# Moving value sums, output products and memory reads between the slots of the last layer

## The chip, the cores and the metric

One core of one Trainium2 chip. The metric is the device time of one execution in microseconds (us), as a median over runs of the same kernel. The core has four compute engines that run side by side: PE (TensorE, the matrix products), DVE (VectorE), ACT (ScalarE) and POOL (GpSimd); SP (SyncE) issues the transfers and, here, also passes on some waits. Results of PE land in PSUM, which this kernel splits into eight banks: four are shared by everything called `g`, two are called `lg`, one `mx`, one `my`.

## What is computed

Four residual layers over x of 2048 rows by 512 columns, 32 heads of 16 columns: linear attention with learned features (A), segment attention with a memory (B), then A and B again with the same weights. Every layer adds its result to x after a layer norm. The change is almost all in B:

```python
for s in range(N):                      # N = 4 segments of L = 512 rows
    qs, ks, vs = q[:, :, s], k[:, :, s], v[:, :, s]
    logits = jnp.einsum("bhqd,bhkd->bhqk", qs, ks) * scale + mask
    p = _softmax(logits, axis=-1)
    a_dot = jnp.einsum("bhqk,bhkd->bhqd", p, vs)
    pq = phi(qs)
    num = jnp.einsum("bhld,bhde->bhle", pq, M)
    den = jnp.einsum("bhld,bhd->bhl", pq, z)[..., None] + 1e-6
    a_mem = num / den
    o = g * a_mem + (1.0 - g) * a_dot   # g = sigmoid(beta), one number per head
    outs.append(o)
    pk = phi(ks)
    M = M + jnp.einsum("bhld,bhle->bhde", pk, vs)
    z = z + jnp.einsum("bhld->bhd", pk)
return o @ wo
```

## The kernel before

**The work of a B layer.** Each segment's 32 heads are worked in eight *half chunks* of four heads. A chunk is 8 heads, that is 128 of the 512 columns, and so two half chunks, `hf` 0 and 1. Half chunks are numbered m = 0 to 31 through a layer; m = 24 to 31 are the last segment's. For each there is a row of five slots (`R = 5`), written m.0 to m.4 with m counted inside the segment (0 to 7).

In every slot PE makes one block of scores into `lg`, ACT takes its exponential into `P`, and POOL cuts `P` along the causal mask (`AFFINE_SELECT`). `lg` holds one block: the next slot's scores wait for this slot's exponential. Beside it PE makes scores for a later half chunk once more, whose row maxima DVE takes (operations with `mask` that write `mxs`): slots .0, .1 and .3 put them in `mx` and `my`, slots .2 and .4 in two `g` tiles (`SPARE`). A transpose `mt<-mxs` then turns the maxima.

**After its five slots a half chunk is summed up.** In slot (m+1).0 PE makes the *value sums* (`weighted`, products of `P` with `v`, 32 matmuls into one `g` tile). ACT *evicts* them from that tile to `U`, scaled by `share`, a number that carries the weight 1 - g of the head (`dve.tensor_scalar(share, ...)` at the start makes it from `gates`). `finish` ("fin" in the tables) lets DVE transpose `U`, take the reciprocal `r` of the sums of exponentials and multiply into `wt`; POOL adds `wt` to `ot`, where the row's share of the memory lies already. That share comes from `reads` ("a0" to "a3", one per chunk): `mem` products into a `g` tile in two rounds, then on DVE a `TENSOR_SCALAR`, a `RECIPROCAL` and a `TENSOR_TENSOR` that reads the bank and writes `ot`.

**The output product.** `convert` ("cv0" to "cv3") transposes a finished chunk of `ot`, ACT copies it to `oh` and DVE or POOL subtracts to get the rest, `ol`. The output product (`out_pair`, "O") takes three products per chunk, `oh` by two parts of `w` and `ol` by one. It runs in `mm3_pair`: two tiles of 128 rows at once, each matmul on 64 of the array's 128 rows, in 24 steps. [...] The change-over is a wait of PE for an empty instruction (`sync.nop`) on SP, which itself waits for PE's last matmul of the part; SP executes in order, so that it stands behind transfers that SP issues before. The last segment's output product is begun early (`early`, "P") on the three chunks that are ready, 18 steps per pair of tiles, and `end` adds the fourth chunk.

**What sets the order.** Four tables written by hand, FIRST, GAPS, LAST and FINAL, name the side work of each slot of a segment: `<` stands ahead of the slot's other work, `O/6` is six steps of the output product, `cv0` the conversion of chunk 0, `pre` the loads of the residual. LAST orders the last segment of the first B layer (layer 1), FINAL that of the second (layer 3, `thin`, the end of the program). In FINAL, rows 2 to 5 hold two output products split by columns into halves of 256 (so 24 steps in each of the four rows).

At the end of the layer m = 31 is summed up: in FINAL by two halves of columns (48 matmuls), ACT evicts each to `U`, `finish` adds both, `end_turn` transposes and splits, `end` multiplies and adds, and the result goes out.

Of the kernel before, what the change touches and what calls it, by code (L numbers as in the profile page):

```python
# [17 lines left out]
DH = 16  # L18
# [72 lines left out]
1.0 <turn <turn <max <a1 | 1.1 fin Q3/6 | 1.2 Q3/6      | 1.3 Q3/6 | 1.4 Q3/6  # L91
2.0 <max <a1 | 2.1 fin O/6          | 2.2 O/6 cv0       | 2.3 O/6 | 2.4 O/6
3.0 <max <a2 | 3.1 fin O/6          | 3.2 O/6           | 3.3 O/6 | 3.4 O/6
4.0 <turn <turn <max <a2 | 4.1 fin O/6 | 4.2 O/6        | 4.3 O/6 cv1 | 4.4 O/6
5.0 <max <a3 | 5.1 fin O/6          | 5.2 O/6           | 5.3 O/6 | 5.4 O/6
6.0 <max <a3 fin pre | 6.1 cv2      | 6.2 P/4           | 6.3 P/9 | 6.4 P/5
7.0 <max | 7.1 fin P/4              | 7.2 P/5           | 7.3 P/4 | 7.4
# [6 lines left out]
def interleave_kernel(ctx, tc, x_in, a_wqkv, a_wphi, a_wo, b_wq, b_wk, b_wv, b_wo, b_beta,  # L104
# [95 lines left out]
    eb = cp.tile([P, H], F32, name="eb")  # L200
    share = cp.tile([P, 8], F32, name="share")
    ones = cp.tile([32, P], F32, name="ones")

    def constants():

        sync.dma_start(out=mask, in_=c_mask)
        sync.dma_start(out=eb, in_=b_beta.unsqueeze(0).broadcast_to([P, H]))
        yield
        yield
        act.activation(eb, eb, AF.Exp, scale=-1.0)  # L210
        dve.tensor_scalar(eb, eb, 1.0, None, op0=ADD)
# [466 lines left out]
    class LayerA:  # L678
# [341 lines left out]
        def pass2(self):  # L1020
# [15 lines left out]
            for i in range(NT):  # L1036
# [31 lines left out]
                if 0 < i <= NT - 4:  # L1068
# [18 lines left out]
    class LayerB:  # L1087
# [261 lines left out]
        def weighted(self, m):  # L1349
# [4 lines left out]
            for w0, w1, kbs in ((0, 256, (0, 1)), (256, 512, (0, 3, 1, 2))) if ends else ((0, 512, (0, 3, 1, 2)),):  # L1354
                pv = PS("g", G)[:, 0 : w1 - w0]
                for kb in kbs:
                    for r in range(2):
                        for e in range(2):
# [6 lines left out]
                            else:  # L1365
# [3 lines left out]
                               lhsT=v[:, kb, h * VW : h * VW + 32], rhs=p[:, q0 - kb * P : w1 - kb * P],  # L1369
                               start=(kb == 0), stop=(kb == kbs[-1]), tile_position=(0, 32 * hh))  # L1370
                U = T2("U", UU)[:, 0 : w1 - w0]
                act.activation(U, pv, AF.Identity, scale=share[:, m % 8 : m % 8 + 1])
                self.U[m].append(U)

        def finish(self, m):
            s, c, hf = m // 8, m % 8 // 2, m % 2
            q0 = 0
            for U in self.U.pop(m):
                n = U.shape[1] // 32
                W = T2("U", UU)[:, 0 : 32 * n]  # L1380
                dve.transpose(out=W, in_=U)
                weigh(self.sums(s, c)[:, q0 : q0 + n, hf : hf + 1],
                      W.rearrange("p (q h e) -> p q h e", q=n, h=1), 0.0, s > 0,
                      dve if m == 8 * NSEG - 1 else pool)
                q0 += n

# [49 lines left out]
        def early(self):  # L1436
# [23 lines left out]

        def end_turn(self):
            s, c = NSEG - 1, NC - 1
            width = 256 if self.thin else 512
            for at in range(0, 512, width):
                S, to = self.turn_sums(s, c, [("oh", OO), ("ol", OO)], ("tb3", TB3), width, at)
                self.split_sums(S, to, dve)

        def end(self):
# [36 lines left out]
        def steps(self, side, after, table_end):  # L1505
# [80 lines left out]
            for s in range(NSEG):  # L1586
                for cell in (FIRST if s == 0 else GAPS if s < NSEG - 1 else table_end).replace("|", "\n").split("\n"):
                    if cell.strip():
                        at_, *what = cell.split()
                        m, j = at_.split(".")  # L1590
                        table[8 * R * s + R * int(m) + int(j)] = what, s
            slots = list(range(*SIDE))
            spent = 0.0
            for k in range(BEGIN, R * N + 1):
# [46 lines left out]
            next(after, None)  # L1641
            self.finish(N - 1)
            for _ in range(4):
                next(early, None)
            for _ in range(2):
                next(after, None)
            self.end_turn()
# [68 lines left out]
```

## Time and profile before

| | |
|---|---|
| runs | 1288.26, 1289.33 and 1291.87 us; median 1289.33 |
| the profiled execution | 1289.33 us, of which the span in the trace is 1287.6 |
| clock of PE granted | 1.00 |
| PE busy | 1253.9 us, 97% of the span |
| DVE, ACT, POOL busy | 83%, 65%, 59% |
| FINAL rows 2 to 5, from PE's value sums of row 2 to those of row 6 | 1213.19 to 1258.09 |
| last value sums of PE end | 1277.44 |

In the rows of the trace a line of "start, us, engine, line, operation, out<-in, count" is one instruction or a run of equal ones, and a bracket at its end is the time the engine was idle just before, with what ended it. Nearly all PE rows bear the line of one helper (L179) and those of the other engines that of another (L157), so a reader goes by the tiles: `g<-P,v` are value sums, `g<-mem,tb` reads, `g<-w,oh`, `g<-w,ol` and `g<-w,x` output products (the conversions of two chunks lie in `x`), `lg<-e,e` scores, and `mx<-e,e`, `my<-e,e`, `g<-e,e` the scores for the maxima. A custom DVE operation with `mask` is a maximum.

### The profile page before, as it was taken

What the parts mean: (1) busy time and instruction counts of PE and PEld (TensorE: products, weight loads), DVE (VectorE), ACT (ScalarE), POOL (GpSimd) and SP (SyncE); (2) the same over time, 40 slices, a digit from 0 to 9 for tenths busy, and PEclk for the clock granted to TensorE, in tenths of its full rate; (3) what the DMA queues carried; (4) which work ended last, traced back from release to release, by engine and by line L of the source; (5) the groups of instructions that cost most, each with busy time, mean ns of one, the idle gap of its engine ahead of it and who ended that gap; (6) DMA issues with size and microseconds to landing.
All of it is one profiled execution on the core that took longest, in us unless ns stands there. A gap on an engine that the chain in (4) does not pass through costs nothing.

```text
span 1287.6 us, 42663 instructions
## 1 busy us (share of the span) xinstructions
PE 1253.9 (97%) x16832; PEld 977.2 (76%) x16832; DVE 1069.0 (83%) x3471; ACT 837.0 (65%) x1258; POOL 753.7 (59%) x1122
## 2 busy tenths in 40 slices
PE   7999999999999999999999999999999999999987
PEld 7887878777777778777668887787877777777765
DVE  5776879699898998999867768887899899899995
ACT  6556446547787787687644434564778967867754
POOL 1668857335667767667324347752456666766653
PEclk9999999999999999999999999999999999999999
DMA  6397348745565545556351102676556545544432
GB/s 216 108 350 259 110 152 259 232 117 151 163 186 150 145 135 145 148 139 170 115 180 51 66 34 83 214 243 173 145 147 203 148 148 138 147 137 118 115 83 83
DMA packets 134423, 196.64 MB, mean 153 GB/s; under 512 B 15440, under 2 KB 61648, under 8 KB 133456
## 3 DMA queue, kind: packets, MB, share of 16 engines
q1 hardware_dynamic: 133408, 193.80, 49.7%
q8 instruction: 134, 2.20, 0.7%
q14 instruction: 65, 0.53, 0.1%
q10 hardware_dynamic: 816, 0.11, 0.1%
HBM read 101.05 MB, written 39.85 MB: 109 GB/s over the span
## 4 chain that ended last, share of the span: by engine, by line
PE 79%; DVE 15%; ACT 2%; issue 1%; DMA 1%; POOL 1%; SPq 0%; DVEq 0%; ACTq 0%; POOLq 0%
PE g L179 61%; PE lg L179 8%; PE g L183 4%; PE mx L179 3%; DVE g L157 3%; DVE mx L157 2%; DVE U L157 2%; DVE my L157 2%; PE my L179 1%; DVE mxs L157 1%; ACT P L157 1%; PE mx L189 1%; DVE es L157 1%; DVE r L157 1%; POOL P L157 1%
## 5 line engine op out<-in xcount | busy, mean ns | idle before, releaser
L157 ACT ACTIVATE P<-lg 128x1024 f32<-128x1024 f32 x316 | 324.2, 1026 | 96.1 <-PE lg L179 76.9
L157 POOL TENSOR_SCALAR_AFFINE_SELECT P<-P 128x256 f32<-128x256 f32 (+1 forms) x448 | 190.0, 441 | 217.3 <-ACT P L157 201.5
L157 DVE CUSTOM_DVE_ANT_0 g<-g,mask 128x128 f32<-128x128 f32 (+3 forms) x392 | 189.5, 538 | 7.3 <-PE g L179 7.0
L157 DVE CUSTOM_DVE_ANT_0 mx<-mx,mask 128x512 f32<-128x512 f32 (+2 forms) x316 | 159.0, 503 | 37.4 <-PE my L179 30.5
L179 PE MATMUL g<-hh,wqk 64*128 64x512 f32 (+1 forms) x960 | 183.6, 392 | 0.4 <-SPq L157 0.2
L179 PE MATMUL g<-w,oh 64*128 64x512 f32 (+2 forms) x848 | 161.8, 380 | 2.6 <-ACT oh L157 2.6
L157 DVE CUSTOM_DVE_ANT_0 my<-my,mask 128x512 f32<-128x512 f32 (+2 forms) x316 | 163.8, 518 | 0.1
L179 PE MATMUL lg<-e,e 64*128 64x512 f32 (+1 forms) x1010 | 146.8, 342 | 7.5 <-ACT P L157 7.5
L179 PE MATMUL g<-P,v 128*32 128x128 f32 (+3 forms) x2064 | 151.7, 433 | 0.2
L157 DVE DVE_READ_ACCUMULATOR2_ANT mxs<- 128x1 f32 x1024 | 143.9, 141 | 0.0
L179 PE MATMUL g<-w,hh 64*128 64x512 f32 (+1 forms) x672 | 142.0, 393 | 0.1
L179 PEld LDWEIGHTS lg<-e,e 64*128 64x128 f32 x1010 | 94.0, 184 | 50.5 <-ACT P L157 19.0
L179 PEld LDWEIGHTS g<-hh,wqk 64*128 64x128 f32 (+1 forms) x960 | 101.1, 185 | 17.2 <-issue 1.0
L179 PEld LDWEIGHTS g<-P,v 128*32 128x32 f32 x2064 | 65.0, 109 | 61.2 <-issue 53.8
L179 PEld LDWEIGHTS g<-w,oh 64*128 64x128 f32 (+1 forms) x848 | 95.6, 186 | 20.2 <-ACT oh L157 3.5
L157 ACT COPY tb<-g 128x512 f32<-128x512 f32 (+1 forms) x132 | 71.1, 575 | 51.5 <-PE g L179 51.3
L179 PE MATMUL g<-hl,wqk 64*128 64x512 f32 (+1 forms) x480 | 102.4, 389 | 0.0
L179 PE MATMUL g<-w,ol 64*128 64x512 f32 (+2 forms) x424 | 100.5, 377 | 0.1
L179 PEld LDWEIGHTS g<-w,hh 64*128 64x128 f32 (+1 forms) x672 | 83.8, 186 | 14.9 <-PE my L179 0.4
L179 PE MATMUL g<-w,hl 64*128 64x512 f32 (+1 forms) x336 | 89.3, 391 | 0.0
L157 POOL TENSOR_TENSOR ta<-tb,ta 128x512 fp32r<-128x512 f32 x60 | 76.2, 1290 | 13.9 <-ACT ta L157 11.0
L179 PE MATMUL g<-e,e 63*128 63x256 f32 (+3 forms) x488 | 83.2, 351 | 0.3 <-issue 0.3
(174 smaller groups left out, 2941.4 us busy)
## 6 DMA issues: line engine op xcount, KB each, us to landing
e<-ta SPq DMA_DIRECT2D x384, 128.0 KB
wqk<-wqk SPq DMA_DIRECT2D x128, 256.0 KB
x<-x SPq DMA_DIRECT2D x48, 256.0 KB
pq<-tb SPq DMA_DIRECT2D x24, 256.0 KB
tb<-pq SPq DMA_DIRECT2D x24, 256.0 KB
x<-xr SPq DMA_DIRECT2D x22, 256.0 KB
xr<-x SPq DMA_DIRECT2D x20, 256.0 KB
x<-in SPq DMA_DIRECT2D x16, 256.0 KB
```

Source lines behind the costliest of these rows:

```text
L157: i = f(*a, **k)
L179: return held(nc.tensor.matmul(*a, **k))
L183: return held(nc.tensor.transpose(*a))
L189: held(nc.tensor.transpose(out, in_[row : row + 64], ident[row : row + 64, row : row + 64], tile_position=(row, 0)))
```

## The change

The tables, `weighted`, `finish` and the end of the layer change, in five parts.

1. **FINAL rows 2 to 5.** The value sums are split over two slots (two of four key blocks in .0, the other two in .1; `parted` lists the half chunks). `fin` goes from .1 to .2. The 24 steps of O go from four slots of 6 to three of 8 (.2, .3, .4), so that the change-overs after steps 6 and 18 now stand in the middle of a slot's steps. The read of each of these rows goes from .0 to .3.
2. **Row 6 of LAST and FINAL.** Value sums in two slots, `fin` from 6.0 to 6.1, the early steps P/4 and P/9 become P/5 and P/8; the first part of P in `mm3_pair` ends after 6 steps instead of 4 (`half`).
3. **The last half chunk (m = 31) of both B layers.** ACT's eviction is left out: DVE transposes straight from PSUM, and the weight is applied in the multiplication (`gate`, kept beside `share`). In FINAL the first half's conversion is done ahead of the second half's, and its second `ol` behind the first result (`low`).
4. **Which engine.** The subtraction of `cv0` and `cv1` in the last segment goes from DVE to POOL (that of `cv2` stays); the addition of `wt` for m = 29 goes from POOL to DVE.
5. **Layers A.** One pair of small scalings, `scale_q`, is issued one step earlier in the second pass.

```diff
 LAST
-6.0 <max <a3 fin pre | 6.1 cv2      | 6.2 P/4           | 6.3 P/9 | 6.4 P/5 v/1
+6.0 <max <a3 pre | 6.1 fin cv2      | 6.2 P/5           | 6.3 P/8 | 6.4 P/5 v/1
 FINAL
-2.0 <max <a1 | 2.1 fin O/6          | 2.2 O/6 cv0       | 2.3 O/6 | 2.4 O/6
-3.0 <max <a2 | 3.1 fin O/6          | 3.2 O/6           | 3.3 O/6 | 3.4 O/6
...
-6.0 <max <a3 fin pre | 6.1 cv2      | 6.2 P/4           | 6.3 P/9 | 6.4 P/5
+2.0 <max | 2.1                      | 2.2 fin O/8       | 2.3 O/8 cv0 a1 | 2.4 O/8
+3.0 <max | 3.1                      | 3.2 fin O/8       | 3.3 O/8 a2 | 3.4 O/8
...
+6.0 <max <a3 pre | 6.1 fin cv2      | 6.2 P/5           | 6.3 P/8 | 6.4 P/5
...
-    def mm3_pair(one, two, kcs=range(NC), closed=True):
+    def mm3_pair(one, two, kcs=range(NC), closed=True, half=None):
-        half = len(terms) // 2
+        half = half or len(terms) // 2
...
         def weighted(self, m):
+                    if m in self.parted and kb == 1:
+                        yield
...
+                if m == 8 * NSEG - 1:
+                    self.U[m].append(pv)
+                    continue
                 U = T2("U", UU)[:, 0 : w1 - w0]
                 act.activation(U, pv, AF.Identity, scale=share[:, m % 8 : m % 8 + 1])
...
+        def last_sums(self):
+            s, c, m = NSEG - 1, NC - 1, 8 * NSEG - 1
+            low = None
+            for n, pv in enumerate(self.U.pop(m)):
+                w = pv.shape[1]
+                q, at = w // 32, w * n
+                W = T2("U", UU)[:, 0:w]
+                dve.transpose(out=W, in_=pv)
+                weigh(self.sums(s, c)[:, at // 32 : at // 32 + q, 1:2], W.rearrange("p (q h e) -> p q h e", q=q, h=1),
+                      0.0, True, dve, gate[:, m % 8 : m % 8 + 1])
+                if low:
+                    low()
+                S, (hi, lo) = self.turn_sums(s, c, [("oh", OO), ("ol", OO)], ("tb3", TB3), w, at)
+                act.copy(hi, S)
+                def low(S=S, hi=hi, lo=lo):
+                    dve.tensor_tensor(out=lo, in0=S, in1=hi.bitcast(F32), op=SUB)
+            return low
...
         def convert(self, s, c):
-            eng = dve if s == NSEG - 1 else pool
+            eng = dve if s == NSEG - 1 and c == NC - 2 else pool
...
+            self.parted = (*(range(N - 7, N - 3) if self.thin else ()), N - 3)
```

**PE, FINAL row 4, slot 4.4.** Before, the scores `lg` are followed by the two score blocks for the maxima and at once by the last six steps of O (two matmuls each):

```order
L179 MATMUL g_21289<-w_15877,ol_20471 128x256
L179 MATMUL g_21288<-w_15877,ol_20471 128x256
L179 MATMUL lg_21374<-e_2112_13208,e_2113_13209 128x256 x4
L179 MATMUL g_21382<-e_2151_13394,e_2150_13393 128x512
L179 MATMUL g_21383<-e_2151_13394,e_2150_13393 128x512
L179 MATMUL g_21288<-w_15877,oh_20024 128x256
```

In the changed kernel the read stands just ahead of that slot's `lg`, and O has eight steps to go:

```order
L179 MATMUL g_21273<-w_15876,oh_20469 128x256
L179 MATMUL g_21272<-w_15876,oh_20469 128x256
L179 MATMUL g_21331<-mem_13202,tb_3351_20506 32x34 x32
L179 MATMUL lg_21368<-e_2111_13207,e_2112_13208 128x256 x4
L179 MATMUL g_21376<-e_2150_13393,e_2149_13392 128x512
L179 MATMUL g_21377<-e_2150_13393,e_2149_13392 128x512
L179 MATMUL g_21273<-w_15877,oh_20469 128x256
```

The read's tile g_21331 and the second tile of the maxima, g_21377, lie in the same bank (with two O tiles and one more tile of maxima, five tiles want four banks), so that g_21377 must wait until DVE has read g_21331.

**DVE, the same place.** Before, a read (`r`, `r`, `ot`) stands early in a row, right behind the turning of the maxima, and no read stands between the maxima of slot .3 and the pair of 512 wide maxima of slot .4; in row 4 only the transpose of `cv1` does:

```order
L157 ISA my_21347,mxs_13204<-my_21347,mask 128x256
L157 ISA mxs_13204 128x1
L157 STREAM_TRANSPOSE U_21372<-ot_20536 128x512
L157 ISA g_21382,mxs_13204<-g_21382,mask 128x512
L157 ISA mxs_13204 128x1
L157 ISA g_21383,mxs_13204<-g_21383,mask 128x512
L157 ISA mxs_13204 128x1
L157 TENSOR_TENSOR x_21371<-U_21372,x_21370 128x512
```

In the changed kernel the read of slot .3 stands between them:

```order
L157 ISA my_21301,mxs_13203<-my_21301,mask 128x256
L157 ISA mxs_13203 128x1
L157 STREAM_TRANSPOSE U_21329<-ot_20535 128x512
L157 TENSOR_SCALAR r_21364<-g_21331 128x16
L157 RECIPROCAL r_21364<-r_21364 128x16
L157 TENSOR_TENSOR ot_21107<-g_21331,r_21364 128x256
L157 ISA g_21376,mxs_13203<-g_21376,mask 128x512
L157 ISA mxs_13203 128x1
L157 ISA g_21377,mxs_13203<-g_21377,mask 128x512
```

What PE waits for at g_21377 is so the `TENSOR_TENSOR ot`, which on DVE stands behind the four 256 wide maxima of the slot and, in the two rows with a conversion, as here, behind its transpose (the row `U_21329<-ot_20535`). The subtraction `x_21371`, which stood ahead of the next row's maxima, has gone to POOL.

**DVE, the end of the program.** Before, both halves of m = 31 are added to `ot` first, from `U` that ACT has evicted, and then turned and split:

```order
L157 STREAM_TRANSPOSE U_21920<-U_21911 128x256
L157 RECIPROCAL r_21922<-U_21920 128x8
L157 TENSOR_TENSOR wt_21924<-U_21920,r_21922 128x128
L157 TENSOR_TENSOR ot_21427<-ot_21427,wt_21924 128x8x16
L157 STREAM_TRANSPOSE tb_3594_21937<-ot_21427 128x256
L157 TENSOR_TENSOR ol_21936<-tb_3594_21937,oh_21935 128x256
L157 STREAM_TRANSPOSE tb_3595_21941<-ot_21427 128x256
L157 TENSOR_TENSOR ol_21936<-tb_3595_21941,oh_21935 128x256
```

In the changed kernel:

```order
L157 STREAM_TRANSPOSE tb_3588_21916<-ot_21540 128x256
L157 STREAM_TRANSPOSE U_21919<-g_21890 128x256
L157 RECIPROCAL r_21921<-U_21919 128x8
L157 SCALAR_TENSOR_TENSOR wt_21923<-U_21919,gate,r_21921 128x128
L157 TENSOR_TENSOR ot_21540<-ot_21540,wt_21923 128x8x16
L157 TENSOR_TENSOR ol_21915<-tb_3588_21916,oh_21914 128x256
L157 STREAM_TRANSPOSE tb_3592_21927<-ot_21540 128x256
L157 TENSOR_TENSOR tb_3539_21672<-g_21941,tb_3539_21672 128x512
L157 TENSOR_TENSOR ol_21915<-tb_3592_21927,oh_21914 128x256
```

The transpose of the first half's sums (`tb_3588`) has moved ahead of the second half's work, the second half is read from the PSUM tile itself, and the first result (`tb_3539`) stands ahead of the last `ol`.

More of the change, by code (lines that the diff above doesn't have):

```diff
@@ L91 @@
 1.0 <turn <turn <max <a1 | 1.1 fin Q3/6 | 1.2 Q3/6      | 1.3 Q3/6 | 1.4 Q3/6
-2.0 <max <a1 | 2.1 fin O/6          | 2.2 O/6 cv0       | 2.3 O/6 | 2.4 O/6
-3.0 <max <a2 | 3.1 fin O/6          | 3.2 O/6           | 3.3 O/6 | 3.4 O/6
-4.0 <turn <turn <max <a2 | 4.1 fin O/6 | 4.2 O/6        | 4.3 O/6 cv1 | 4.4 O/6
-5.0 <max <a3 | 5.1 fin O/6          | 5.2 O/6           | 5.3 O/6 | 5.4 O/6
-6.0 <max <a3 fin pre | 6.1 cv2      | 6.2 P/4           | 6.3 P/9 | 6.4 P/5
+2.0 <max | 2.1                      | 2.2 fin O/8       | 2.3 O/8 cv0 a1 | 2.4 O/8
+3.0 <max | 3.1                      | 3.2 fin O/8       | 3.3 O/8 a2 | 3.4 O/8
+4.0 <turn <turn <max | 4.1          | 4.2 fin O/8       | 4.3 O/8 cv1 a2 | 4.4 O/8
+5.0 <max | 5.1                      | 5.2 fin O/8       | 5.3 O/8 a3 | 5.4 O/8
+6.0 <max <a3 pre | 6.1 fin cv2      | 6.2 P/5           | 6.3 P/8 | 6.4 P/5
 7.0 <max | 7.1 fin P/4              | 7.2 P/5           | 7.3 P/4 | 7.4
@@ L201, in interleave_kernel @@
     share = cp.tile([P, 8], F32, name="share")
+    gate = cp.tile([P, 8], F32, name="gate")
     ones = cp.tile([32, P], F32, name="ones")
@@ L214, in constants @@
         for j in range(4):
-            dve.tensor_copy(share[32 * j : 32 * j + 32, :].rearrange("p (c f) -> p c f", f=2),
+            dve.tensor_copy(gate[32 * j : 32 * j + 32, :].rearrange("p (c f) -> p c f", f=2),
                             gates[32 * j : 32 * j + 32, 0, :].rearrange("p (c j f) -> p j c f", j=4, f=2)[:, j])
-        dve.tensor_scalar(share, share, -1.0, bd[:, 24:25], op0=ADD, op1=MUL)
+        dve.tensor_scalar(share, gate, -1.0, bd[:, 24:25], op0=ADD, op1=MUL)
         dve.tensor_scalar(share, share, 1.0, None, op0=ADD)
@@ L552, in out_pair, with weigh @@
         yield
-    def weigh(out, p, eps, add, eng=pool):
+    def weigh(out, p, eps, add, eng=pool, part=None):
         n, G = out.shape[1], out.shape[2]
@@ L567, in weigh @@
         t = T2("wt", 1, shape=(P, n, G, DH))
-        dve.tensor_tensor(out=t, in0=p[:, :, :, 0:DH], in1=rb, op=MUL)
+        if part is None:
+            dve.tensor_tensor(out=t, in0=p[:, :, :, 0:DH], in1=rb, op=MUL)
+        else:
+            dve.scalar_tensor_tensor(out=t, in0=p[:, :, :, 0:DH], scalar=part, in1=rb, op0=MUL, op1=MUL)
         eng.tensor_tensor(out=out, in0=out, in1=t, op=ADD)
@@ L1081, in pass2 @@
                         yield from transposed(3)
+                    if i == NT - 4:
+                        for f in factors:
+                            scale_q(*f)()
+                        factors = []
                 elif i > NT - 4:
@@ L1373, in weighted @@
                 self.U[m].append(U)
+            yield
         def finish(self, m):
             s, c, hf = m // 8, m % 8 // 2, m % 2
[L1377 to L1385, printed above, removed]
+            U, = self.U.pop(m)
+            W = T2("U", UU)
+            dve.transpose(out=W, in_=U)
+            weigh(self.sums(s, c)[:, :, hf : hf + 1], W.rearrange("p (q h e) -> p q h e", q=16, h=1), 0.0, s > 0,
+                  dve if m == 8 * NSEG - 3 else pool)
+        def last_sums(self):
[15 more added lines that the diff above has]
+            return low
         def turn_sums(self, s, c, tags, src, width=512, at=0):
@@ L1449, in early @@
                 yield from mm3_pair(side(0), side(1), range(NC - 1),
-                                    t == 0 or not self.thin)
+                                    t == 0 or not self.thin, 6)
                 def end(po=po, xs=self.xe[t : t + 2]):
@@ L1459, in early, with end @@
                 yield
[L1461 to L1468, printed above, removed]
+        def end(self, low):
             s = NSEG - 1
@@ L1479, in end @@
                 sync.dma_start(out=self.xdst[4 * s + t], in_=self.xe[t])
+                if low:
+                    low()
+                    low = None
         def opening(self):
@@ L1591, in steps @@
                         table[8 * R * s + R * int(m) + int(j)] = what, s
+            self.parted = (*(range(N - 7, N - 3) if self.thin else ()), N - 3)
+            values = {}
             slots = list(range(*SIDE))
@@ L1621, in steps @@
                 if k % R == 0 and 0 <= k // R - 1 < N:
-                    self.weighted(k // R - 1)
+                    values = self.weighted(k // R - 1)
+                    next(values)
+                elif k % R == 1 and k // R - 1 in self.parted:
+                    next(values)
                 for f in self.rows:
@@ L1641, in steps @@
             next(after, None)
[L1642 to L1647, printed above, removed]
+            low = self.last_sums()
+            if not self.thin:
+                for _ in range(4):
+                    next(early, None)
+                for _ in range(2):
+                    next(after, None)
+                low()
+                low = None
             for _ in early:
@@ L1650, in steps @@
             next(after, None)
-            self.end()
+            self.end(low)
             for f in aside[0]:
```

## The prediction

> **What bounds the kernel now.** I read the page's busy shares and chain first, then busy time by stage, then the rows of PE and DVE over the last 100 us.
>
> ```profile
> span 1287.6 us, 42663 instructions
> PE 1253.9 (97%) x16832; PEld 977.2 (76%) x16832; DVE 1069.0 (83%) x3471; ACT 837.0 (65%) x1258; POOL 753.7 (59%) x1122
> PE 79%; DVE 15%; ACT 2%; issue 1%; DMA 1%; POOL 1%; SPq 0%; DVEq 0%; ACTq 0%; POOLq 0%
> ```
>
> PE is nearly always busy and the chain is mostly PE, so a change can only take out PE's few gaps. The change leaves PE's products as they are, 7567 rows before and after. The gaps stand at the last layer's end; its windows run from value sums to value sums (rows 2 to 7):
>
> ```profile
> core 0: us, PE busy (x) PEld busy (x) DVE busy (x) ACT busy (x) POOL busy (x), PEclk, DMA share, GB/s
> 1213.19:1225.41 12.22, 9.88 (x195) 7.23 (x182) 11.50 (x45) 9.62 (x14) 9.53 (x13) 1.00 0.31 71
> 1225.41:1236.12 10.71, 9.69 (x179) 7.15 (x177) 10.34 (x47) 6.04 (x8) 5.52 (x12) 1.00 0.33 90
> 1236.12:1247.04 10.92, 9.87 (x195) 7.22 (x182) 10.22 (x42) 6.29 (x10) 4.67 (x10) 1.00 0.45 122
> 1247.04:1258.09 11.05, 9.76 (x175) 7.17 (x174) 10.84 (x44) 7.01 (x9) 6.07 (x12) 1.00 0.22 72
> 1258.09:1267.93 9.84, 8.55 (x86) 5.47 (x84) 4.33 (x13) 5.26 (x7) 3.60 (x9) 1.00 0.24 85
> 1267.93:1277.44 9.51, 9.51 (x124) 6.20 (x122) 3.57 (x8) 6.36 (x10) 4.07 (x9) 1.00 0.00 1
> ```
>
> In rows 2 to 5 (44.90 us in all) PE is idle 5.70 us and DVE only 2.00, so DVE sets the pace there. PE's gaps that the change aims at, in both B layers:
>
> ```profile
> 622.67 0.77 PE L179 MATMUL g<-mem,tb 128*32 128x34 f32 x64 [0.63 <-DVE mxs L157]
> 638.54 0.56 PE L179 MATMUL lg<-e,e 64*128 64x256 f32 x4 [1.28 <-ACT P L157]
> 663.62 0.74 PE L179 MATMUL g<-w,oh 128*128 128x512 f32 x2 [1.24 <-ACT oh L157]
> ...
> 1224.67 0.77 PE L179 MATMUL g<-mem,tb 128*32 128x34 f32 x64 [0.94 <-DVE mxs L157]
> ...
> 1262.16 0.56 PE L179 MATMUL lg<-e,e 64*128 64x256 f32 x4 [1.28 <-ACT P L157]
> ...
> 1280.16 0.73 PE L179 MATMUL g<-w,oh 128*128 128x512 f32 x2 [1.35 <-ACT oh L157]
> ```
>
> **FINAL rows 2 to 5.** Here the sign is decided. The order puts the read of slot .3 on DVE behind the four 256 wide maxima, and PE's second 512 wide block of slot .4 into the bank that this read empties. Today DVE runs late and nobody minds. DVE in row 5:
>
> ```profile
> 1247.81 0.29 DVE L157 CUSTOM_DVE_ANT_0 mx<-mx,mask 128x128 f32<-128x128 f32 x1
> ...
> 1249.30 0.84 DVE L157 STREAM_TRANSPOSE mt<-mxs 32x32 f32<-32x32 f32 x4
> 1250.07 0.12 DVE L157 TENSOR_SCALAR r<-g 128x16 f32<-128x16 f32 x1
> ...
> 1250.86 0.69 DVE L157 CUSTOM_DVE_ANT_0 mx<-mx,mask 128x512 f32<-128x512 f32 x1
> ...
> 1252.11 0.70 DVE L157 STREAM_TRANSPOSE U<-U 128x512 f32<-128x512 f32 x1
> ...
> 1253.48 0.29 DVE L157 CUSTOM_DVE_ANT_0 g<-g,mask 128x128 f32<-128x128 f32 x1
> ...
> 1254.97 0.47 DVE L157 CUSTOM_DVE_ANT_0 mx<-mx,mask 128x256 f32<-128x256 f32 x1
> ...
> 1256.50 0.73 DVE L157 CUSTOM_DVE_ANT_0 g<-g,mask 128x512 f32<-128x512 f32 x1
> ...
> 1257.97 0.62 DVE L157 STREAM_TRANSPOSE mt<-mxs 32x32 f32<-32x32 f32 x3
> ```
>
> and PE's rows of the same slots:
>
> ```profile
> 1253.55 0.40 PE L179 MATMUL g<-w,oh 64*128 64x256 f32 x4
> 1253.79 0.28 PE L179 MATMUL g<-w,ol 64*128 64x256 f32 x2
> ...
> 1254.68 0.51 PE L179 MATMUL lg<-e,e 64*128 64x256 f32 x4 [0.25 <-ACT P L157]
> 1255.02 0.64 PE L179 MATMUL g<-e,e 63*128 63x512 f32 x2
> 1255.25 0.53 PE L179 MATMUL g<-w,oh 64*128 64x256 f32 x3
> ```
>
> PE makes the 512 wide blocks at 1255.02; DVE gets to them at 1256.50. This lead of PE is what the new wait eats. From a row's first maximum to the end of its read, by differences of starts: maxima 1.49, turning 0.77, 512 wide pair 1.25, the next four maxima 1.49, `U` 1.37, 256 wide 1.53, read 0.79: 8.69. DVE will also stand some 0.26 before the four maxima in `g`, since PE has to go through the value sums, two `lg` and ACT's eviction to get there (my estimate from the same rows): 8.95. Behind the read comes work of PE that now waits for it: the block 0.23 (1255.02 to 1255.25), eight steps of O, a change-over, `lg` 0.34 (1254.68 to 1255.02) and the next maxima's first product, 0.3 with its handing on; I allow 0.1 for PE's start. Four matmuls of O, two steps, take 0.24 (1253.55 to 1253.79), so eight steps 0.94. The change-over in mid-stream does not occur before. The nearest row stands between two slots:
>
> ```profile
> 908.76 0.49 PE L179 MATMUL g<-hh,wqk 64*128 64x512 f32 x2
> ...
> 909.92 0.50 PE L179 MATMUL g<-hh,wqk 64*128 64x512 f32 x2 [0.21 <-SPq L157]
> ```
>
> From 909.25, the first part's end, to 909.92 are 0.67, the high end; the low end is 0, if the array drains beside the next load. I take 0.29: the trace's ends lie a drain behind the next start (908.76 plus 0.49 against a stride of 0.23 there, so 0.26), and SP adds a few hundredths. Behind the read: 0.1 + 0.23 + 0.94 + 0.29 + 0.34 + 0.3 = 2.2. A row without a conversion so takes 11.15, where before row 3 took 10.71 and row 5 11.05: +0.54 together. The transpose of a conversion adds 0.67 on DVE ahead of the read. Row 4: 11.15 + 0.67 + 0.3, since its change-over stands on SP behind six transfers (below): 12.1 against 10.92, +1.2. Row 2 has also ACT's 2.6 us more of other work ahead of the eviction (9.62 in its window against 7.01); I let 0.6 of it through: 12.4 against 12.22, +0.2. Sum: **+1.9**, between −3.2 (no wait on the bank: DVE's own work, the 8.69, 1.3 for the last pair and 0.1 of reading out, is 10.1 a row, 10.8 with a transpose, 41.7 against 44.9) and +5 (eight change-overs at 0.67 where four at 0.29 are counted, 4.2, and another 0.9 of SP's transfers).
>
> ```profile
> 1236.76 0.88 SPq L157 DMA_DIRECT2D out<-mmq  x1
> 1237.74 5.00 SPq L157 DMA_DIRECT2D e<-ta  x6
> ```
>
> The value sums' second slot costs nothing by itself, since `lg` and its exponential now run between their halves. O's second tile in .2 waits for ACT's eviction of its bank; DVE's maxima and `U` (1.49 and 1.37) cover it, and without that cover it would be some 0.4 a row. The read's products are 0.74 on PE (1224.67 to 1225.41), moved from ahead of the value sums to ahead of the last `lg`, where DVE's 256 wide maxima cover them; no transfer moves with them.
>
> **The subtractions on POOL.** On DVE they took 1.41 in row 2, on POOL one like it 1.29:
>
> ```profile
> 1200.79 1.29 POOL L157 TENSOR_TENSOR ol<-U,oh 128x512 fp32r<-128x512 f32 x1
> ...
> 1222.53 1.41 DVE L157 TENSOR_TENSOR x<-U,x 128x512 fp32r<-128x512 f32 x1
> ...
> 1265.01 0.69 DVE L157 TENSOR_TENSOR ol<-U,oh 128x512 fp32r<-128x512 f32 x1 [0.69 <-ACT oh L157]
> ```
>
> POOL is busy 4.67 of row 4's 10.92, so it has room; its result is wanted rows later. In layer 3 DVE's relief goes into the bank wait (counted above); in layer 1, where no such wait is made, PE's 0.63 at 622.67 closes: −0.6 (0 to −0.63). The same subtraction on DVE took 1.41 in row 2, where POOL is busy 9.53 of 12.22, and 0.69 in row 6 at 3.60 of 9.84: beside POOL it costs up to 0.72 more, and the move may turn that round, POOL's instruction holding up DVE's next ones (a rival below; nothing in the sum, since no row shows POOL holding up DVE's maxima, most of what follows).
>
> [...]
>
> **Row 6.** Today ACT evicts `U` ahead of the exponential and PE stands 1.28 in each layer. With half the value sums behind the next `lg`, the exponential runs first. `fin` and the conversion then come one slot later, which I let leave a quarter of the gap: −1.0 in layer 3 and, since the P steps there gain a change-over, −0.6 in layer 1 (each 0 to −1.28).
>
> **Row 7.** P's change-overs leave the slots' borders too: one on PE's path in each layer, +0.3 (0 to +0.67).
>
> **The end.** Between the last value sums (1277.44) and the last addition stands one serial chain:
>
> ```profile
> 1277.47 0.47 ACT L157 ACTIVATE U<-g,share 128x256 f32<-128x256 f32 x1 [1.04 <-PE g L179]
> ...
> 1279.23 0.44 DVE L157 STREAM_TRANSPOSE tb<-ot 128x256 f32<-128x256 f32 x1
> ...
> 1281.74 2.48 DVE L157 TENSOR_TENSOR tb<-g,tb 128x512 f32<-128x512 f32 x4
> ```
>
> It ends 6.78 behind, at 1284.22. PE's products for it start at 1280.16 after 1.35 of idle. In the changed order the first half is split before the second is summed, so PE goes on without that idle at 1278.81; the first tile's third product needs the `ol` that stands on DVE behind the second half's four operations, whose like here take 1.25 up to the transposition at 1279.23, so just in time. All moves up by 1.35, and the additions, which waited on DVE for both `ol`, by some 0.15 more: −1.5 (0 if the chain only changes engines, to −1.9). In layer 1 the same chain leaves 1.24 at 663.62; without an eviction like the 0.47 here −0.5 (0 to −1.24).
>
> **Sum.** Layer 3: +1.9 − 1.0 + 0.3 − 1.5 = −0.3. Layer 1: −0.6 − 0.6 + 0.3 − 0.5 = −1.4, and it arrives in full, since layer 2 begins on PE's results. `scale_q` a step earlier: nothing. Together −1.7; I say −1.5, 1287.8, for the profiled execution, whose 1289.33 is also the median.
>
> **The rivals.** *The bank wait is hidden* (faster). If DVE reaches the read sooner, because its lag at the start of each row shrinks, rows 2 to 5 give −3.2 instead of +1.9: −1.7 − 5.1 = −6.8, about 1282.5; with half of that gain 1285. For it speaks that DVE's work per row falls, with two subtractions gone; against it, that PE's path behind the read is fixed at 2.2. *The change-overs* (slower). Sixteen now stand in mid-stream. At the 0.67 of 909.92 on all of them, where I have 0.29 on some six, it is 16 × 0.67 − 6 × 0.29 = +9 at most; with a quarter of them covered by waits on DVE and ACT +6.3, and 1294. It decides from 5.4 on, with eleven of them bare (1287.8 to 1293.2). For it: in row 4 SP issues transfers for 5.00 us in one go; against: of the 0.67 only 0.21 were idle, other products ran between. *POOL holds DVE*: four subtractions at 0.72 each on the path, +2.9, and layer 1's −0.6 lost: 1291.3, no change by itself. The rows' 1.41 speaks for it, against it that only `wt` and the reads' operations follow it closely. [...] *The ends gain nothing*, because the chain only moves to another engine: 0 in place of −2.0, 1289.8, still no change.
>
> **How the numbers follow.** What this kernel's measurement can tell is about 0.3%, 3.9 us: faster is below 1285.5, slower above 1293.2. No change: 0.45 by the sum above, 0.08 with the ends idle, 0.05 with POOL holding DVE, together 0.58. The bank wait hidden, wholly or mostly: 0.32. The change-overs dear: 0.10. The range takes in the hidden wait down to 1283, and upward the ends at 0 and change-overs half as dear as the rival's, 1291.5. With the likeliest alone it is 1285.5 to 1290.
>
> **What would show it.** Right: in rows 2 to 5 PE's `g<-e,e` of slot .4 waits for DVE `ot`, and rows last 11 to 12.5; at row 6 the 1.28 is gone; the last value sums end near 1278.5 and the last addition 5.3 later. Wrong: rows under 10.6 (the wait hidden), SPq as releaser of PE with over 0.5 each, or a gap before P's chunk 2 in row 6 as long as the old one.

## The result, and the profile after

The changed kernel takes 1296.51 us (median of 5 runs, 1296.01 to 1300.94) against 1289.33: the ratio is 1.0057, 95% interval 1.0044 to 1.0069. It is slower by 7.2 us, outside the forecast range. The page of its profiled execution:

```profile
span 1294.8 us, 42660 instructions
PE 1263.4 (98%) x16832; PEld 976.7 (75%) x16832; DVE 1068.7 (83%) x3469; ACT 835.5 (65%) x1255; POOL 758.5 (59%) x1124
PE 82%; DVE 12%; POOL 2%; issue 2%; ACT 1%; DMA 1%; SPq 1%; DVEq 0%; POOLq 0%; ACTq 0%
```

PE shows 9.5 us more busy time for the same products, but that alone tells little: the runs e2 and e6 below show 1259.9 and 1261.8 and have no such loss. Where the 7.2 went is read from the starts of the value sums, stage by stage (before, after, and how far after lies behind, worked out before rounding):

| value sums of | before | after | behind |
|---|---|---|---|
| layer 1, row 4 | 611.32 | 610.82 | −0.51 |
| layer 1, row 5 | 623.41 | 622.29 | −1.12 |
| layer 1, row 7 | 644.82 | 643.83 | −0.99 |
| layer 1, m = 31 | 657.03 | 656.78 | −0.26 |
| layer 3, row 2 | 1213.19 | 1212.68 | −0.51 |
| row 3 | 1225.41 | 1227.60 | +2.19 |
| row 4 | 1236.12 | 1240.32 | +4.20 |
| row 5 | 1247.04 | 1253.87 | +6.83 |
| row 6 | 1258.09 | 1266.23 | +8.14 |
| row 7 | 1267.93 | 1276.03 | +8.10 |
| m = 31 | 1274.58 | 1282.96 | +8.39 |
| end of the span | 1287.6 | 1294.8 | +7.2 |

FINAL rows 2 to 5 lose 8.65; the end gives 1.2 back; all else sums to little. The busy times of those four windows, then PE's waits in them (waited for by, us in total, times, longest):

```profile
core 0: us, PE busy (x) PEld busy (x) DVE busy (x) ACT busy (x) POOL busy (x), PEclk, DMA share, GB/s
1212.68:1227.60 14.92, 11.11 (x179) 7.54 (x177) 11.39 (x43) 9.69 (x16) 11.29 (x16) 0.96 0.23 51
1227.60:1240.32 12.72, 11.57 (x178) 7.35 (x176) 10.24 (x42) 5.83 (x8) 4.65 (x10) 0.91 0.27 61
1240.32:1253.87 13.55, 10.84 (x179) 7.36 (x177) 10.94 (x43) 6.77 (x10) 6.36 (x11) 1.00 0.46 134
1253.87:1266.23 12.36, 11.20 (x239) 7.67 (x238) 11.04 (x46) 6.57 (x10) 5.37 (x11) 1.00 0.06 17
```

```profile
PE g L179 <- DVE ot L157: 5.3, 4, 2.5
PE g L179 <- SPq L157: 1.7, 1, 1.7
PE g L179 <- ACT U L157: 0.8, 1, 0.8
PE lg L179 <- ACT P L157: 0.3, 1, 0.3
```

DVE's busy time has hardly grown, but it no longer fills its rows: 14.92 with 11.39 of work. The wait on the bank that the read empties (`DVE ot`) stands once in each of the four rows, and PE's mean granted clock is 0.96 and 0.91 in the first two windows, 1.00 in the others. Row 2, in POOL's, DVE's and PE's rows, shows why its wait is the longest:

```profile
1219.68 1.49 POOL L157 TENSOR_SCALAR tb<-tb 128x512 f32<-128x512 f32 x1
1221.25 1.27 POOL L157 TENSOR_TENSOR tb<-tb,tb 128x512 f32<-128x512 f32 x1
1222.49 0.72 POOL L157 TENSOR_TENSOR ot<-ot,wt 128x256 f32<-128x256 f32 x1
```

```profile
1223.25 0.71 DVE L157 STREAM_TRANSPOSE U<-ot 128x512 f32<-128x512 f32 x1 [1.13 <-POOL ot L157]
...
1224.34 0.42 DVE L157 TENSOR_TENSOR ot<-g,r 128x256 f32<-128x256 f32 x1
```

```profile
1224.91 0.47 PE L179 MATMUL g<-e,e 63*128 63x512 f32 x1 [2.49 <-DVE ot L157]
```

With `fin` one slot later, POOL takes up two operations on `tb` ahead of the addition to `ot`; the transpose of `cv0` waits for that addition on DVE, the read stands behind the transpose, and PE behind the read: four engines in one chain, 2.49 us. What came next is the clock. Two windows of 3.41 us of this trace, the one with the wait and the next:

```profile
1223.11:1226.53 3.42, 1.53 (x19) 1.34 (x21) 2.86 (x8) 0.82 (x2) 2.70 (x5) 1.00 0.00 0
1226.53:1229.94 3.41, 3.41 (x28) 1.30 (x24) 2.19 (x12) 1.57 (x3) 1.78 (x3) 0.50 0.77 175
```

PE was busy 1.53 of 3.42, and then ran at a clock of 0.50 for 3.41 us. Of that window 1.07 lie at the end of row 2 and the rest in row 3, whose first 16 value sums took 2.36, against 1.28 in row 4:

```profile
1227.60 2.36 PE L179 MATMUL g<-P,v 128*32 128x512 f32 x16
...
1240.32 1.28 PE L179 MATMUL g<-P,v 128*32 128x512 f32 x16
```

So by estimate up to 1.7, half of the window, was lost. In row 4 the change-over in slot .2 stands behind SP's transfers, SP's row and then PE's:

```profile
1242.22 5.08 SPq L157 DMA_DIRECT2D e<-ta  x6
```

```profile
1247.41 0.51 PE L179 MATMUL g<-w,oh 64*128 64x256 f32 x4 [1.74 <-SPq L157]
```

### The profile page after: what moved, and what is told of

Same layout as the page of the kernel before. It is cut to its first block, busy times and chain, and to the rows that moved or that the text cites. A ratio compares the mean times of both kernels' runs of the same rounds, so it can differ in the third digit from the quotient of the medians.

```text
span 1294.8 us, 42660 instructions
## 1 busy us (share of the span) xinstructions
PE 1263.4 (98%) x16832; PEld 976.7 (75%) x16832; DVE 1068.7 (83%) x3469; ACT 835.5 (65%) x1255; POOL 758.5 (59%) x1124
## 4 chain that ended last, share of the span: by engine, by line
PE 82%; DVE 12%; POOL 2%; issue 2%; ACT 1%; DMA 1%; SPq 1%; DVEq 0%; POOLq 0%; ACTq 0%
PE g L179 63%; PE lg L179 8%; PE g L183 4%; PE mx L179 4%; DVE g L157 2%; DVE U L157 2%; PE my L179 2%; DVE mx L157 2%; DVE my L157 1%; PE mx L189 1%; ACT P L157 1%; DVE mxs L157 1%; POOL P L157 1%; SPq L157 1%; DVE r L157 1%
## 5 line engine op out<-in xcount | busy, mean ns | idle before, releaser
L179 PE MATMUL g<-w,oh 64*128 64x512 f32 (+2 forms) x848 | 166.7, 386 | 5.0 <-SPq L157 1.7
L157 POOL TENSOR_TENSOR ta<-tb,ta 128x512 fp32r<-128x512 f32 x60 | 76.3, 1292 | 14.0 <-ACT ta L157 6.4
```

Of the source, the lines that this page charges most:

```text
L157: i = f(*a, **k)
L179: return held(nc.tensor.matmul(*a, **k))
```

## The experiments

The theory after this trace: the place of the read makes the loss (a wait on its bank, in row 2 lengthened by POOL, and the clock behind it); the rivals are the change-overs, the split value sums, and the other parts. The ratios below are to runs of the kernel before on the same chip, whose medians there were 1290.69 to 1291.12.

**Rows 2 to 5 back (e1).** FINAL rows 2 to 5 as before, the rest of the change kept:

```diff
-            self.parted = (*(range(N - 7, N - 3) if self.thin else ()), N - 3)
+            self.parted = (N - 3,)
```

> The changed kernel with FINAL rows 2 to 5 as before (value sums in one slot there, O/6 in four slots, reads in .0); the rest of the change stays. If rows 2 to 5 hold the whole loss: 1288.0 (1287 to 1289.5), with the end 1.2 shorter than before. If row 6, row 7 or layer 1 lose too: 1291 or more.

Measured 1288.12, ratio 0.9982 (0.9972 to 0.9993). The whole loss lies in the four rows; the rest of the change is a gain.

**The reads back in .0 (e2), or in .2 (e6).**

```diff
-2.0 <max | 2.1                      | 2.2 fin O/8       | 2.3 O/8 cv0 a1 | 2.4 O/8
+2.0 <max <a1 | 2.1                  | 2.2 fin O/8       | 2.3 O/8 cv0 | 2.4 O/8
...
-2.0 <max | 2.1                      | 2.2 fin O/8       | 2.3 O/8 cv0 a1 | 2.4 O/8
+2.0 <max | 2.1                      | 2.2 fin O/8 a1    | 2.3 O/8 cv0 | 2.4 O/8
```

The first pair is e2, the second e6; rows 3 to 5 are edited alike.

> The changed kernel with only the reads of FINAL rows 2 to 5 back in slot .0. If the bank wait behind the read is the loss: PE's waits for DVE ot (5.3 us) go, PE's clock stays at 1.00 in row 3 (1.7 us), and some 0.5 a row comes back as waits for DVE mxs: 1290.5 (1289.5 to 1292). If the change-overs or the split value sums are the loss: 1294.5 or more.

> The changed kernel with the reads of FINAL rows 2 to 5 one slot earlier, behind O in .2: the same eight g tiles a row in the same order, but on DVE the read stands ahead of the four 256 wide maxima and of the conversion. If the place on DVE makes the bank wait: PE's waits for DVE ot go from 5.3 to under 0.5 and the clock stays at 1.00, 1289.5 (1288 to 1291), ratio 1.000. If the read costs PE wherever it stands among the slots: 1294 or more, 1.004.

Measured: e2 1288.82, ratio 0.9988 (0.9976 to 1.0001); e6 1290.13, ratio 0.9992 (0.9982 to 1.0002). Value sums, O/8 and change-overs are in both as in the changed kernel. PE's waits in the same rows, e2 and then e6:

```profile
PE g L179 <- SPq L157: 1.6, 1, 1.6
PE g L179 <- DVE mxs L157: 1.0, 1, 1.0
PE g L179 <- ACT U L157: 0.7, 1, 0.7
```

```profile
PE g L179 <- SPq L157: 1.2, 1, 1.2
PE g L179 <- ACT U L157: 0.8, 1, 0.8
PE lg L179 <- ACT P L157: 0.3, 1, 0.3
```

No `DVE ot` in either, and the clock stays at 1.00 in these executions (mean granted clock 1.000 in both). e2 is a little faster than its forecast range (1289.5 to 1292). e6 tells most: one slot earlier the read comes ahead of the 256 wide maxima and the conversion on DVE, and the wait is gone, though it still stands among the slots of O. So it is the read's place; without it the other parts make no loss that the ratios show.

**The read alone (e11).** The kernel before with only the reads of these rows in .3, rows 3 to 5 alike:

```diff
-2.0 <max <a1 | 2.1 fin O/6          | 2.2 O/6 cv0       | 2.3 O/6 | 2.4 O/6
+2.0 <max | 2.1 fin O/6              | 2.2 O/6 cv0       | 2.3 O/6 a1 | 2.4 O/6
```

> The kernel before with one part of the change alone: the reads of FINAL rows 2 to 5 in .3. If the bank wait is enough by itself: PE waits for DVE ot in each row, 1 to 2.5 each, with half clock behind where a window of 3.41 us is filled to about half: 1293 to 1296, ratio 1.003 to 1.005. If it needs the split value sums or O/8: within 1 of before, 1.000.

Measured 1295.22, ratio 1.0029 (1.0018 to 1.0041). PE waits for `DVE ot` four times, 6.4 us in all; its rows with the waits of rows 2 to 4, and the two windows after which the clock went to 0.50:

```profile
1223.51 0.76 PE L179 MATMUL g<-e,e 63*128 63x512 f32 x1 [2.58 <-DVE ot L157]
...
1237.60 0.47 PE L179 MATMUL g<-e,e 63*128 63x512 f32 x1 [1.08 <-DVE ot L157]
...
1249.68 0.66 PE L179 MATMUL g<-e,e 63*128 63x512 f32 x1 [1.75 <-DVE ot L157]
```

```profile
1219.07:1222.48 3.41, 1.86 (x78) 1.35 (x75) 3.41 (x13) 2.29 (x3) 3.33 (x4) 1.00 0.16 37
...
1246.37:1249.79 3.42, 1.67 (x75) 1.21 (x74) 3.35 (x15) 1.97 (x3) 1.66 (x4) 1.00 0.03 5
```

One part of the change, put alone into the kernel before, makes a loss of the same kind, about half as large by the ratios (1.0029 and 1.0057). In this execution rows 2 to 5 lose 7.85, with three windows at half clock, since the first halving lasted two (1222.48 to 1229.31); its mean granted clock is 0.996.

**The conversion later (e3).** `cv0` in 3.3 instead of 2.3:

```diff
-2.0 <max | 2.1                      | 2.2 fin O/8       | 2.3 O/8 cv0 a1 | 2.4 O/8
-3.0 <max | 3.1                      | 3.2 fin O/8       | 3.3 O/8 a2 | 3.4 O/8
+2.0 <max | 2.1                      | 2.2 fin O/8       | 2.3 O/8 a1 | 2.4 O/8
+3.0 <max | 3.1                      | 3.2 fin O/8       | 3.3 O/8 cv0 a2 | 3.4 O/8
```

> The changed kernel with the conversion of chunk 0 one row later (3.3 instead of 2.3). If the 2.49 us wait of row 2 comes from POOL's late addition to ot, on which this conversion waits on DVE ahead of the read: row 2's wait falls to about 1, row 3's rises to about 1.6, PE's clock stays at 1.00: 1293.3 (1292 to 1294.5). If the wait has another cause: 1296.

Measured 1295.86, ratio 1.0034 (1.0021 to 1.0047): above the range in us. But the kernel before took 1290.76 on that chip and not 1289.33, and as a ratio the forecast, 1293.3 to 1289.33, is 1.0031. PE's waits of rows 2 and 3 and two windows:

```profile
1223.81 0.47 PE L179 MATMUL g<-e,e 63*128 63x512 f32 x1 [0.63 <-DVE ot L157]
1236.52 0.46 PE L179 MATMUL g<-e,e 63*128 63x512 f32 x1 [1.70 <-DVE ot L157]
```

```profile
1234.52:1237.93 3.41, 1.62 (x18) 1.13 (x17) 3.19 (x12) 1.53 (x2) 2.37 (x4) 1.00 0.00 0
...
1248.17:1251.59 3.42, 1.79 (x18) 1.27 (x18) 3.35 (x12) 1.53 (x2) 2.46 (x4) 1.00 0.02 5
```

The waits moved as expected (2.49 to 0.63, and 1.70 in row 3), so POOL's addition does lengthen row 2's. But PE's clock was halved twice in this execution instead of never (0.50 from 1237.93 and from 1251.59, 3.41 us each), by estimate up to 1.7 us each. The two of the twelve runs whose mean granted clock is 1.000 took 1293.32 and 1293.90, inside the range. The waits ahead of the two halvings, 1.70 and 1.54 (row 4), each fell wholly into one window.

**The change-overs (e4, e12, e5).** At a change-over the two tiles of `mm3_pair` swap the halves of PE's rows, in O after steps 6 and 18 of the 24. e4 is the changed kernel with O in 6, 12, 6 steps; e12 the kernel before with O in 4, 8, 8, 4; e5 is e1 with the early steps P/4, P/9, P/5 and without `half=6`, so that P's change-overs stand between slots. In this order:

```diff
-3.0 <max | 3.1                      | 3.2 fin O/8       | 3.3 O/8 a2 | 3.4 O/8
+3.0 <max | 3.1                      | 3.2 fin O/6       | 3.3 O/12 a2 | 3.4 O/6
...
-3.0 <max <a2 | 3.1 fin O/6          | 3.2 O/6           | 3.3 O/6 | 3.4 O/6
+3.0 <max <a2 | 3.1 fin O/4          | 3.2 O/8           | 3.3 O/8 | 3.4 O/4
...
-6.0 <max <a3 pre | 6.1 fin cv2      | 6.2 P/5           | 6.3 P/8 | 6.4 P/5
+6.0 <max <a3 pre | 6.1 fin cv2      | 6.2 P/4           | 6.3 P/9 | 6.4 P/5
```

> The changed kernel with O in 6, 12 and 6 steps in .2, .3, .4, so that the change-overs fall between slots as before. If they are the loss: eight times 0.25 and most of row 4's 1.74 on SP go: 1293 (1292 to 1294). If the bank wait sets the pace, PE only waits longer there and the four change-overs ahead of the read give nothing: 1295 to 1296.

> The kernel before with one part alone: O of FINAL rows 2 to 5 as 4, 8, 8, 4 steps, so that both change-overs of each row stand in the middle of a slot's steps. If each costs its 0.25 and row 4's stands 1.6 behind SP's transfers: 2 to 3.5 more, ratio 1.002 to 1.003. If PE's waits for the exponential cover them: 1.0003 or less.

> The kernel of e1 (rows 2 to 5 as before) with the early steps P/4, P/9, P/5 as before, so that P's change-overs stand between slots again in both layers. If they cost 0.25 to 0.35 each in mid-stream (eight of them): 1.5 to 2.5 less than e1, ratio 0.9968 (0.9960 to 0.9975); layer 1's row 7 then loses its 0.7 no more. If they are covered: as e1, 0.9982.

Measured: e4 1295.34, ratio 1.0033 (1.0021 to 1.0046); e12 1290.96, ratio 0.9999 (0.9990 to 1.0009); e5 1286.98, ratio 0.9968 (0.9955 to 0.9980), against 0.9982 of e1. In e4 the four waits for `DVE ot` remain (5.3 in all), and its rows 2 to 5 lose 5.18 where the changed kernel's lose 8.65. Row 4 is 1.57 shorter, without the wait on SP. From the end of the bank wait to the next value sums row 4 takes 1.65 instead of 2.24, since two steps of O and a change-over have left that stretch. So the change-overs, with these steps, are up to two fifths of the loss, and the larger part stays without them; as ratios to 1289.33 e4's two forecasts, 1293 and 1295 or more, are 1.0028 and 1.0044, and the result lies nearer the first. In e12, where no read stands in .3, O's change-overs alone cost nothing that shows in the medians. In its profiled execution row 4's did stand behind SP, 1.97, and by the rows behind it half clock followed (four `g<-w,oh` took 0.63 at 1245.93 and at 1248.17, and 0.40 at 1249.97; the mean granted clock is 0.999):

```profile
1245.20 0.72 PE L179 MATMUL g<-w,oh 64*128 64x256 f32 x4 [1.97 <-SPq L157]
```

That execution's rows 2, 3 and 5 lie +0.04, +0.23 and −0.44 from the kernel before, and row 4 +3.4; the timed runs show no such loss on average, so how often row 4 is hit is open. P's change-overs do cost where nothing else is waited for: layer 1's row 7 is 0.69 longer in e1 than before and 0.01 in e5. Between e1 and e5 the intervals overlap; the stage is what shows it.

**The other parts (e7, e9, e10).** e7 is the kernel before with only the new end (`last_sums`, `gate`, `end(low)`); e9 is e5 with row 6 wholly as before (the addition of `wt` for m = 29 is on POOL again too); e10 is e5 with the subtractions back on DVE (the first two pairs of lines are e9, the last e10):

```diff
-6.0 <max <a3 pre | 6.1 fin cv2      | 6.2 P/4           | 6.3 P/9 | 6.4 P/5
+6.0 <max <a3 fin pre | 6.1 cv2      | 6.2 P/4           | 6.3 P/9 | 6.4 P/5
-            self.parted = (N - 3,)
+            self.parted = ()
...
-            eng = dve if s == NSEG - 1 and c == NC - 2 else pool
+            eng = dve if s == NSEG - 1 else pool
```

> The kernel before with only the end of the B layers changed (no eviction of the last half chunk, first half split first). By the theory that the end gains what the changed kernel's trace shows: 1.2 in layer 3 and 0.3 in layer 1, ratio 0.9988 (0.9980 to 0.9996). If the end only moves its chain: 1.000.

> The kernel of e5 with row 6 wholly as before in both layers (value sums in one slot, fin in 6.0): the end, the subtractions of cv0 and cv1 on POOL and scale_q are left of the change. If splitting row 6 gives nothing, since the late conversion makes PE wait for oh instead (1.2 in e5): 0.4 less than e5 in layer 3 and nothing in layer 1, ratio 0.9965. By the prediction's step (1.0 and 0.6 gained): 1.6 more than e5, 0.998.

> The kernel of e5 with the subtractions of cv0 and cv1 back on DVE. If their move to POOL is what shortened rows 2 to 5 by 1.7 and layer 1's row 5 by 0.6: 2.3 more than e5, ratio 0.9985. If POOL's longer subtraction holds DVE up as much: as e5, 0.9968.

Measured: e7 1288.38, ratio 0.9978 (0.9966 to 0.9991), a little more than expected; by the stages it gains 0.65 in layer 1 (from the value sums of m = 31 to the first product of `oh`) and 1.2 in layer 3. e10 1288.31, ratio 0.9983 (0.9973 to 0.9994) against e5's 0.9968. These intervals overlap, but rows 2 to 5 are as long as before in e10 and 1.67 shorter in e5. e9 1285.96, ratio 0.9961 (0.9948 to 0.9973): the fastest of all, 0.4% under the kernel before. Rows 2 to 5 of e9:

```profile
1212.31:1223.52 11.21, 9.79 (x194) 7.19 (x182) 10.53 (x46) 9.77 (x15) 8.71 (x13) 1.00 0.32 72
1223.52:1234.23 10.71, 9.68 (x179) 7.12 (x177) 10.03 (x44) 6.12 (x9) 7.33 (x14) 1.00 0.39 101
1234.23:1245.14 10.91, 9.85 (x194) 7.21 (x181) 10.21 (x44) 6.29 (x10) 4.92 (x10) 1.00 0.45 122
1245.14:1255.54 10.40, 9.30 (x177) 6.83 (x174) 9.99 (x44) 6.36 (x9) 5.99 (x12) 1.00 0.19 59
```

Rows 2 and 5 are 1.01 and 0.65 shorter than before, 3 and 4 the same. The last one, **e8**, tried whether the split value sums are worth anything once bank wait and mid-stream change-overs are gone (P/4, P/9, P/5 too; rows 3 to 5 alike):

```diff
-2.0 <max | 2.1                      | 2.2 fin O/8       | 2.3 O/8 cv0 a1 | 2.4 O/8
+2.0 <max <a1 | 2.1                  | 2.2 fin O/6       | 2.3 O/12 cv0 | 2.4 O/6
```

> The changed kernel with the reads back in .0 (as e2), O in 6, 12 and 6 steps, and P/4, P/9, P/5, so that neither the bank wait nor a change-over in mid-stream is left. If both are costs: 0.9988 of e2 less eight change-overs of O and eight of P at 0.25, and less half of row 4's 1.6 on SP: ratio 0.996 (0.995 to 0.997). If the change-overs are covered once the bank wait is gone: as e2, 0.9988.

Measured 1287.98, ratio 0.9970 (0.9958 to 0.9981). Its rows 2 to 5 gain 1.62, no more than e5's 1.67 without split value sums. Against e2, at 0.9988, row 4 is 1.02 shorter, since the wait on SP is gone.

## Why the prediction was wrong, point by point

**The sign turned on the bank wait, which was found, and sized at +1.9 where rows 2 to 5 lost 8.65.** The order named the right wait, and rows 3 and 5 show it at 0.97 each. The step that failed is the sum of a row. It was built as 8.95 on DVE, from the first maximum to the end of the read, and 2.2 behind. Row 5 has neither a conversion nor half clock, and from its first maximum at 1253.97 DVE comes to the next one behind the read after 9.48; it stood 0.52 ahead of the four maxima in `g` where 0.26 was estimated:

```profile
1258.26 0.30 DVE L157 CUSTOM_DVE_ANT_0 g<-g,mask 128x128 f32<-128x128 f32 x1 [0.52 <-PE g L179]
...
1263.45 0.69 DVE L157 CUSTOM_DVE_ANT_0 g<-g,mask 128x512 f32<-128x512 f32 x1
```

In rows 3 and 4 the part behind the read is 2.57 (row 4: 1251.40 to 1253.97 on DVE). So some 0.5 in each row, and 0.4 more in rows 2 to 4, are sizes taken too small. The rest differs by row:
- Row 2, 12.4 forecast and 14.92 measured. Only ACT's work ahead of the eviction was counted; POOL's two `tb` operations ahead of `ot`, and so 1.13 of DVE standing still ahead of the read, were not. The moved `fin` was costed at nothing without asking what stands ahead of it on POOL. `wt` took 0.4 more beside POOL's `tb`. Half clock took about 0.45: from the end of the bank wait to the next value sums it is 2.69, in row 4 2.24. Of the 0.6 allowed for ACT hardly any came.
- Row 3, 11.15 and 12.72. Half clock took about 0.7 on the path: the second half of the value sums starts 2.96 behind the first, where it is 2.29 in row 4. A clock under 1.00 was in no term, since the trace of before has none within the program (mean granted clock 1.000).
- Row 4, 12.1 and 13.55. PE's change-over stood 1.74 behind SP, where 0.3 was taken, though the 5.00 us of transfers were in view. DVE's work covers a part; 0.76 shows on DVE ahead of the read:

```profile
1248.48 0.43 DVE L157 CUSTOM_DVE_ANT_0 mx<-mx,mask 128x256 f32<-128x256 f32 x1 [0.76 <-PE my L179]
```

- Row 5, 11.15 and 12.36. The window ends behind a read that stayed in 6.0, while its own had left its front: about 0.7 that was overlooked; the other 0.5 is the 9.48.

**The change-overs' price** was nearly right, by two neighbouring rows of layer 1, row 7, of the changed kernel:

```profile
648.61 0.39 PE L179 MATMUL g<-w,ol 64*128 64x512 f32 x2
649.10 0.73 PE L179 MATMUL g<-w,oh 64*128 64x512 f32 x4
```

They start 0.49 apart where one step takes 0.23, so 0.26 against 0.29 forecast; the two steps behind take 0.57 (649.10 to 649.67) instead of 0.46, 0.1 more. The rival that made the whole loss out of them was wrong: e12 shows no loss from them, and e4 keeps 5.18 of 8.65 without them. But behind the bank wait they add to it, and there row 4's was priced too low.

**The subtractions on POOL** were undervalued: nothing in layer 3 forecast, where the move is worth 1.7 as soon as the bank wait is away (e5 against e10); −0.6 in layer 1, measured −0.61 (from −0.51 to −1.12 behind). The rival that POOL holds DVE fell with e10. Still, in the changed kernel's row 2 a `wt` beside POOL's `tb` took 0.83 (at 1219.74), against 0.43 in rows 4 and 5; if POOL's subtractions do the like, it is less than their move saves, 1.67 in rows 2 to 5.

**Row 6** was wrong in both layers: −1.0 and −0.6 forecast, −0.04 and +0.12 measured. The gap at the exponential goes, but the conversion comes a slot later and PE waits for `oh` instead, in e5:

```profile
1265.28 0.74 PE L179 MATMUL g<-w,oh 64*128 64x512 f32 x4 [1.20 <-ACT oh L157]
```

A quarter of the gap had been left for that; in e5 it was nearly all of it. In the changed kernel this wait is 0.45 (at 1273.58), and two of P's change-overs stand in layer 3's row 6, which the −1.0 did not count. e9, without the split, is as fast or faster.

**Row 7**: +0.3 forecast, +0.29 in layer 3, +0.73 in layer 1, where two of P's change-overs stand bare, and not one. **The end**: −1.5 and −0.5 forecast, −1.2 and −0.64 measured. In layer 1 the first product of `oh` starts 5.95 behind the value sums of m = 31 (656.78 to 662.73), and started 6.59 behind before. The chain is shortened as described, but in layer 3 its second half's split comes late, so that the additions end 1291.52, 5.7 behind the last value sums, where 5.3 was forecast and 6.78 measured before:

```profile
1289.45 2.07 DVE L157 TENSOR_TENSOR tb<-g,tb 128x512 f32<-128x512 f32 x3
```

**The chances.** The case "slower" had 0.10, tied to the change-overs alone, which are the smaller part of the loss. The likeliest case's own upper bound for rows 2 to 5, +5, is the sum of its two additions, 4.2 and 0.9, without the +1.9 that they come on top of: with it, it is +7.0. Neither has a term for POOL's chain or for half clock.

## What to carry to other kernels

When more tiles are live than there are banks, find which read frees the bank that the next product wants, and follow that read back over every in-order queue it stands on: here DVE, then POOL behind a conversion. The place of one short operation on DVE, one slot earlier or later, was worth 8 to 9 us by the ratios (1.0057 against 0.9992 and 0.9988), while splitting or spreading PE's own products gained nothing. And take each part of a change by itself: here the end and the move to POOL, with `scale_q`, give 0.4% when the others are left away.

## What the runs showed of the hardware that was not expected

In rows 2 to 5 of the changed kernel's trace PE's granted clock was 1.00, but for one stretch of 3.41 us at 0.50 (1226.53 to 1229.94). In e3 and e11 the stretches at 0.50 are as long: 1237.93 to 1241.35 and 1251.59 to 1255.00 in e3, 1249.79 to 1253.20 in e11, and from 1222.48 in e11 two of them in a row. Laid end to end with these stretches, the windows of the same length ahead of a halving had PE busy for 0.45 (changed kernel), 0.48 and 0.52 (e3), 0.49 and 0.55 (e11) of their length; a window at 0.61 (changed kernel) was followed by full clock. The changed kernel's two are the row at 1223.11 above and this one, with 2.08 of 3.42:

```profile
1243.59:1247.01 3.42, 2.08 (x28) 1.48 (x20) 2.88 (x12) 1.60 (x2) 0.82 (x3) 1.00 0.57 132
1247.01:1250.42 3.41, 3.01 (x97) 2.83 (x97) 2.55 (x11) 1.03 (x1) 1.51 (x3) 1.00 0.43 97
```

So each halving shown had a window ahead of it in which PE was busy for about half. The busy share alone does not settle every case: in e11's window at half clock from 1222.48 PE was busy for 2.38 of 3.41, and half clock went on behind it, by its 32 value sums from 1226.44, which took 3.75 where those from 1239.24 took 2.36.

Waits of 1.54 to 2.58 us in a dense stream stood ahead of these halvings, and each halved window cost, by estimate, up to half of its 3.41, 1.7 more. Not every wait of that length had a halving behind it: the changed kernel's 1.74 behind SP, up to 1247.41, lies across the border of two windows at 1247.01, and full clock followed. It also differs from one execution to the next: the mean granted clock of e3's twelve runs is 0.995 to 1.000. The runs of e11 give an idea of the shares: its two of six at a mean granted clock of 1.000 took 1293.20 and 1293.75, so some 2.4 of its 4.1 us stay without a halving. For the changed kernel itself no run at 1.000 is on record.
